# Block-sparse attention and a feed-forward layer on one core: attention in 64x64 quadrants of the TensorE array

## The chip, the cores and the metric

One core of a Trainium2 chip. The time is the device time of one execution in microseconds (us), and a kernel's time is the median of its runs. TensorE is called PE, its weight loads PEld, VectorE DVE, ScalarE ACT, GpSimd POOL and SyncE SP. PEclk is the clock that the throttle granted to PE: 1.0 is full speed, 0.5 half.

## The reference, cut to what matters

```python
# q, k, v: 4 batches x 8 heads x 768 positions x 64, float32
scores_l = q @ k.T / 8                      # kept where |i - j| < 16
scores_s = q @ k_sum.T / 8 + log(32)        # k_sum: maximum over blocks of 32 keys
a = softmax(concat([scores_l masked, scores_s]))
attn = a @ concat([v, v_sum])               # v_sum: mean over blocks of 32 keys
x = attn, heads side by side                # 3072 x 512
h = x @ w_in                                # 512 -> 2048
out = (h * clip(h + 3, 0, 6) / 6) @ w_out   # 2048 -> 512
```

## The kernel before

The feed-forward layer (`hp`, `op`) is the bulk of PE's work: 912 products with full 128x128 weights. Attention is laid between its steps by a hand-made plan of slots. A head is 64 wide, half of PE's rows, so the kernel puts two heads (a pair `p`) on the 128 rows and keeps them apart with block-diagonal operands, half of them zeros: `kbd`, `vbd`, `obd`.

```python
def Sl(b, p, lo, hi):                       # local scores of one pair
    sp = ps_s.tile([128, 512], F32, tag="s", name="sl")
    for i in range(hi - lo):
        t = lo + i
        nc.tensor.matmul(sp[:, i*WIN:(i+1)*WIN], kbd[p][:, t], qT[p][:, ...], start=True, stop=True)
    nc.scalar.activation(a, sp[...], AF.Exp, scale=scl)
    nc.vector.tensor_tensor(a, a, mask, op=ALU.mult)
# [...] Ss: scores with the block summaries, `ss`; exponentials `asum`
def AV(b, p, half):                         # x of one pair, half of the sequence
    nc.tensor.matmul(num[:], vst[p], asm[:], start=True, stop=False)       # block sums of v
    for i, (t, lo, hi, off) in enumerate(bl):                              # 7 key blocks
        nc.tensor.matmul(num[:, lo:hi], vbd[p][:, t], a[:, t, off:off+hi-lo], ...)
    nc.tensor.matmul(den[:], osum[p % 2], asm[:], start=True, stop=False)
    # [...] three products of a with the block-diagonal ones obd, into den
    nc.scalar.activation(lg[:], den[:], AF.Ln)
    nc.scalar.activation(lg[:], lg[:], AF.Exp, scale=-1.0)
    nc.vector.tensor_tensor(xt[s][:, p], num[:], lg[:], op=ALU.mult)
```

The start is written out by hand. `K` and `Tq` transpose k and q of a pair on PE, `busy` are warm-up products on zeros, and `vsum0` makes the block sums of v for the first batch on PE, from float32 (`vps`). The sums need only v, so they sit where q and k of the next pair are still on their way:

```python
K(0, 0)
busy(busy_n, 4)
Tq(0, 0, 0)
vsum0(0)                      # 12 float32 products, 24 instructions in the trace
vcast(0)
K(0, 1)
S_first(0)
vsum0(1, 0, NK // 2)
Tq(0, 1, 0)
vsum0(1, NK // 2, NK)
# [...] pairs 2 and 3 in the same way, then AV(0, 0..3, 0)
```

For later batches DVE makes the sums from v's rows, which come in one transfer for four heads: 4 x 24 blocks on 96 partitions.

```python
def load_vrows(b, g):
    vr_t[b, g] = ld.tile([RS, PCS, w + 8], F32, tag="vr", name="vr", bufs=2)       # RS = 96
    nc.gpsimd.dma_start(out=vr_t[b, g][:, :, 0:w],
                        in_=v[b, 4*g:4*g + 4].rearrange("h (n c t) d -> (h n) c (t d)", c=PCS, n=NB))
```

The softmax here doesn't subtract the row's maximum and nothing guards it: scores larger than these inputs give would overflow.

## Time and profile before

| | before |
|---|---|
| median of 4 runs | 250.66 us (250.37 to 250.72) |
| span of the profiled run | 248.7 us |
| first dense product (`hp`) starts | 25.48 us |
| from there to the last matmul (244.63) | 219.2 us |
| granted clock | 1.0 from 6.9 us to the end of the work |
| busy: PE, DVE, ACT | 236.2, 151.4, 162.2 us |

The table is to be read in two pieces. Up to 25.48 us the core loads, transposes and makes the first x; nothing dense can run before that, so a microsecond lost there is a microsecond of the whole. After it PE is the bound, and attention's instructions count only by the PE time that they take between dense products, and by the waits that they bring. The prediction below shows the lines for both. One more line, of the DMA part of the page (target and source, queue, kind, number, KB each, median us to landing):

```profile
vr<-in_v_dram POOLq DMA_DIRECT2D x6, 768.0 KB, 9.0
```

### The profile page before, as it was taken

To read this page: it belongs to the slowest core of one execution; us is meant where nothing else is said; L and a number is where in the kernel's file an instruction comes from. 1 tells how busy PE (TensorE), PEld (TensorE's weight loads), DVE (VectorE), ACT (ScalarE), POOL (GpSimd) and SP (SyncE) were. 2 spreads that over 40 slices of the span, in tenths; PEclk is the share of its full clock that TensorE was granted. 3 is DMA by queue.
4 is the path that set the end of the run, shared out by engine and by line. 5 is a ranking of instruction groups with operands and counts; after the bars stand their busy time and mean duration, and the time that the engine had idled before them with its cause. 6 is when DMAs were issued, how large, how long until landed. Compare 5 with 4: busy or idle time off the path is not lost.

```text
span 248.7 us, 5021 instructions
## 1 busy us (share of the span) xinstructions
PE 236.2 (95%) x1927; PEld 139.5 (56%) x1950; DVE 151.4 (61%) x354; ACT 162.2 (65%) x316; POOL 67.4 (27%) x101
## 2 busy tenths in 40 slices
PE   7999999999999999769999999999999999999993
PEld 2897566445555656445655555566565555555553
DVE  5598576325579749999863977766444544444300
ACT  8587798427968879865866565777765555555411
POOL 8655005626950216596341200000000000000000
PEclk9999999999999999999999999999999999999999
DMA  6999998999999699999999912110110111111012
GB/s 120 203 173 205 206 193 132 205 248 157 223 155 162 190 213 102 133 128 224 139 180 138 104 33 76 42 45 3 43 42 3 42 42 45 42 42 41 19 71 84
DMA packets 75448, 28.90 MB, mean 116 GB/s; under 512 B 63904, under 2 KB 71328, under 8 KB 75424
## 3 DMA queue, kind: packets, MB, share of 16 engines
q0 software_dynamic: 52752, 17.57, 62.0%
q1 hardware_dynamic: 22672, 11.01, 19.4%
q8 instruction: 15, 0.25, 0.4%
q14 instruction: 9, 0.07, 0.1%
HBM read 31.98 MB, written 6.29 MB: 154 GB/s over the span
## 4 chain that ended last, share of the span: by engine, by line
PE 69%; DVE 19%; ACT 5%; DMA 3%; issue 2%; ACTq 0%; DVEq 0%; POOLq 0%
PE op L443 27%; PE hp L426 26%; DVE g L430 4%; PE num L395 3%; PE sl L357 2%; PE num L393 2%; DVE red L322 2%; DMA kb<-in_k_dram 2%; DVE red L301 2%; ACT r L429 2%; DVE x L413 2%; PE ss L367 2%; PE den L399 2%; DVE kbd L300 2%; DVE kbd L318 2%
## 5 line engine op out<-in xcount | busy, mean ns | idle before, releaser
L426 PE MATMUL hp<-x,win 128*128 128x384 bf16 x512 | 103.2, 326 | 2.0 <-DVE g L430 1.8
L429 ACT ACTIVATE r<-hp,half_c 128x384 f32<-128x384 f32 x128 | 73.2, 580 | 46.4 <-PE hp L426 43.6
L430 DVE SCALAR_TENSOR_TENSOR g<-r,hp 128x384 bf16<-128x384 f32 x128 | 69.8, 552 | 52.2 <-ACT r L429 51.9
L443 PE MATMUL op<-wout,g 128*128 128x512 bf16 x345 | 93.5, 379 | 1.2 <-issue 0.3
L426 PEld LDWEIGHTS <-win 128*128 128x128 bf16 x512 | 47.7, 97 | 37.7 <-issue 5.4
L443 PEld LDWEIGHTS <-g 128*128 128x128 bf16 x368 | 35.2, 98 | 30.7 <-issue 0.6
L413 DVE TENSOR_TENSOR x<-num,lg 128x384 bf16<-128x384 f32 x32 | 17.8, 556 | 21.4 <-ACT lg L412 19.7
L120 POOL DMA_DIRECT2D vbd<-in_v_dram x24 | 18.1, 762 | 33.7 <-PE num L395 21.2
L411 ACT ACTIVATE lg<-den 128x384 f32<-128x384 f32 x32 | 15.7, 492 | 14.8 <-PE den L409 7.2
L360 ACT ACTIVATE at<-sl 128x376 bf16<-128x376 f32 (+2 forms) x48 | 22.2, 486 | 3.9 <-PE sl L357 3.7
L361 DVE TENSOR_TENSOR at<-at,mask 128x376 bf16<-128x376 bf16 (+2 forms) x48 | 16.2, 349 | 2.6 <-ACT at L360 2.3
L412 ACT ACTIVATE lg<-lg 128x384 f32<-128x384 f32 x32 | 16.8, 525 | 0.8
L447 ACT COPY ot<-op 128x512 f32<-128x512 f32 x23 | 13.2, 586 | 5.9 <-PE op L443 5.7
L357 PE MATMUL sl<-qT,kbd 128*128 128x94 bf16 x192 | 14.6, 206 | 2.0 <-DVE kbd L300 1.2
L357 PEld LDWEIGHTS <-kbd 128*128 128x128 bf16 x192 | 11.7, 98 | 8.3 <-issue 1.9
L395 PEld LDWEIGHTS <-vbd 128*128 128x128 bf16 x224 | 12.9, 98 | 5.3 <-issue 1.6
L113 POOL DMA_DIRECT2D qb<-in_q_dram x16 | 13.5, 868 | 5.3 <-DMA vr<-in_v_dram 4.2
L395 PE MATMUL num<-at,vbd 128*128 128x94 bf16 (+2 forms) x224 | 14.1, 199 | 0.0
L113 POOL DMA_DIRECT2D kb<-in_k_dram x16 | 13.6, 883 | 0.0
L402 PE MATMUL den<-at,obd 128*128 128x384 bf16 x32 | 10.7, 333 | 0.5 <-DVE at L361 0.5
L393 PE MATMUL num<-asum,vst 96*128 96x384 bf16 x32 | 10.5, 327 | 0.5 <-DVE x L413 0.3
L399 PE MATMUL den<-asum,osum 96*128 96x384 bf16 x32 | 10.4, 325 | 0.0
(83 smaller groups left out, 204.7 us busy)
## 6 DMA issues: line engine op xcount, KB each, us to landing
out_dram<-ot SPq DMA_DIRECT2D x23, 256.0 KB, 2.3
vr<-in_v_dram POOLq DMA_DIRECT2D x6, 768.0 KB, 9.0
vbd<-in_v_dram POOLq DMA_DIRECT2D x24, 96.0 KB, 4.9
win<-in_moe_w_in_dram POOLq DMA_DIRECT2D x4, 512.0 KB, 9.2
wout<-in_moe_w_out_dram POOLq DMA_DIRECT2D x4, 512.0 KB, 17.0
vf<-in_v_dram SPq DMA_DIRECT2D x8, 192.0 KB, 7.2
kb<-in_k_dram POOLq DMA_DIRECT2D x16, 96.0 KB, 6.2
qb<-in_q_dram POOLq DMA_DIRECT2D x16, 96.0 KB, 6.2
```

The costliest lines, as they stand in the source:

```text
L113: nc.gpsimd.dma_start(out=t[:, :, j], in_=src[b, 2 * p + j].rearrange("(s p) d -> p s d", p=128))
L120: nc.gpsimd.dma_start(out=vall[rows, p, lo:hi, rows], in_=v[b, 2 * p + j].rearrange("(n k) d -> k n d", k=KB)[:, lo:hi])
L357: nc.tensor.matmul(sp[:, i * WIN:(i + 1) * WIN], kbd[p][:, t], qT[p][:, PAD - HALO + t * KB:PAD - HALO + t * KB + WIN], start=True, stop=True)
L360: nc.scalar.activation(a, sp[:, 0:n * WIN].rearrange("p (n c) -> p n c", c=WIN), AF.Exp, scale=scl)
L361: nc.vector.tensor_tensor(a, a, mask[:].unsqueeze(1).to_broadcast([128, n, WIN]), op=ALU.mult)
L395: nc.tensor.matmul(num[:, lo:hi], vbd[p][:, t], a[:, t, off:off + hi - lo], start=False, stop=(i == len(bl) - 1))
L412: nc.scalar.activation(lg[:], lg[:], AF.Exp, scale=-1.0)
L413: nc.vector.tensor_tensor(xt[s][:, p], num[:], lg[:], op=ALU.mult)
L426: nc.tensor.matmul(hp[:], w_in_sb[:, kt, ft * 128:(ft + 1) * 128], xt[t][:, kt], start=(kt == 0), stop=(kt == NP - 1))
L429: nc.scalar.activation(r[:], hp[:], AF.Relu, bias=half_c[:], scale=1.0 / 6.0)
L430: last_g[0] = nc.vector.scalar_tensor_tensor(gt[t][:, ft], r[:], 1.0, hp[:], op0=ALU.min, op1=ALU.mult)
L443: nc.tensor.matmul(op[:], gt[t][:, ft, ts * 128:(ts + 1) * 128], w_out_sb[:, ft], start=(ft == 0), stop=(ft == NFT - 1))
```

## The change

Intent: use the 128x128 array as four 64x64 quadrants, one head each, so that no product multiplies zeros, and the block-diagonal copies need not be made. Four heads are one group `g`. Each row half of the array writes its own PSUM bank. With that go one instruction for twice the columns on ACT, a rearranged order of the start, and v's rows in 32-row places, because the summaries of a head now sit at multiples of 32 partitions.

```diff
 def Sl(...):
-    sp = ps_s.tile([128, 512], F32, tag="s", name="sl")
+    sp = ps_a.tile([128, 2, 512], F32, tag="a", name="sl")
     for i in range(n):
-        nc.tensor.matmul(sp[:, i*WIN:...], kbd[p][:, t], qT[p][:, ...])
+        for r, c in QUAD:                     # ((0,0), (1,1), (0,1), (1,0))
+            p = 2 * g + (r + c) % 2
+            nc.tensor.matmul(sp[quarter(c), r, i*WIN:...], kT[p][quarter(r), t*KB:...], qT[p][quarter(r), ...])
 # AV becomes AVd (den, Ln, Exp) and AVn (num, x), each for a group; in both
+    for c in range(2):                        # block sums: 64 rows x 128 columns
+        nc.tensor.matmul(num[:, c, 0:HALF], vst[b % 2][g][quarter(c)], asm[quarter(c)], start=True, stop=False)
+    for i, (t, lo, hi, off) in enumerate(bl): # values: quarters
+        for r, c in QUAD:
+            nc.tensor.matmul(num[quarter(r), c, lo:hi], vb[b % 2][quarter(c), 2*g + r, t], a[quarter(c), r, t, ...])
 def load_vrows(b, g):
-    nc.gpsimd.dma_start(out=vr_t[b, g][:, :, 0:w], in_=v[b, 4*g:4*g + 4]...)
+    for i in range(4):
+        nc.gpsimd.dma_start(out=vrow[g][SR*i:SR*i + NB, :, 0:w], in_=v[b, 4*g + i]...)
 # the start
 K(0, 0)
 busy(busy_n, 4)
 Tq(0, 0, 0)
-vsum0(0)
 K(0, 1)
-S_first(0)
-vsum0(1, 0, NK // 2)
 Tq(0, 1, 0)
-vsum0(1, NK // 2, NK)
+S_first(0)
 K(0, 2)
 Tq(0, 2, 0)
+vsum0(0)                                      # 24 float32 products, 48 instructions in the trace, 128 weight columns
 Ss(0, 0, 0, HALF)
 K(0, 3)
 Tq(0, 3, 0)
+AVd(0, 0, 0)
+S_first(1)
+vsum0(1)                                      # 24 more
 # [...] then Ss, AVn(0), AVd(1), AVn(1)
```

Cut: the vb and kT buffers, the transposes in groups, the slots of the plan.

## The prediction

> **What bounds the kernel now.** I read the page's busy shares and chain first, then the groups by shape, then TensorE (PE) in order of time, then busy time by stage.
>
> ```profile
> PE 236.2 (95%) x1927; PEld 139.5 (56%) x1950; DVE 151.4 (61%) x354; ACT 162.2 (65%) x316; POOL 67.4 (27%) x101
> ...
> PE 69%; DVE 19%; ACT 5%; DMA 3%; issue 2%; ACTq 0%; DVEq 0%; POOLq 0%
> ```
>
> PE is 95% busy and 69% of the chain that ended last. DVE's 19% of the chain says that some stages hang on VectorE.
>
> ```profile
> L426 PE MATMUL hp<-x,win 128*128 128x384 bf16 x512 | 103.2, 326 | 2.0 <-DVE g L430 1.8
> L443 PE MATMUL op<-wout,g 128*128 128x512 bf16 x345 | 93.5, 379 | 1.2 <-issue 0.3
> ...
> L357 PE MATMUL sl<-qT,kbd 128*128 128x94 bf16 x192 | 14.6, 206 | 2.0 <-DVE kbd L300 1.2 <-ACT at L360 0.8
> ```
>
> Matmuls overlap, so the busy column double counts: what one costs is the step from its start to the next start. A merged row of n matmuls gives it as (length - one duration)/(n-1).
>
> ```profile
> 34.43 0.37 PE L357 MATMUL sl<-qT,kbd 128*128 128x94 bf16 x5
> 34.64 0.81 PE L426 MATMUL hp<-x,win 128*128 128x384 bf16 x4
> ```
>
> That is (370-206)/4 = 41 ns for 94 columns and (810-326)/3 = 161 ns for 384: 2.4 columns a nanosecond. The dense part is then 512 x 0.162 = 83 us plus 384 x 0.216 = 83 us (368 matmuls of 512 columns and 32 halves; 23 records are missing in the count above), 166 us together, and the change does not touch it. One call of the attention's second product (one head pair, half the sequence) is read from its neighbours' starts:
>
> ```profile
> 24.61 0.33 PE L393 MATMUL num<-asum,vst 96*128 96x384 bf16 x1
> 24.78 0.42 PE L395 MATMUL num<-at,vbd 128*128 128x79 bf16 x7
> 25.06 0.32 PE L399 MATMUL den<-asum,osum 96*128 96x384 bf16 x1
> 25.22 0.34 PE L402 MATMUL den<-at,obd 128*128 128x384 bf16 x1
> ...
> 25.48 3.26 PE L426 MATMUL hp<-x,win 128*128 128x384 bf16 x16
> ```
>
> 25.48 - 24.61 = 0.87 us, 32 times: 27.8 us. Local scores: 192 x 0.0417 = 8.0 us. Summary scores: 32 x 0.162 = 5.2 us. So 41.0 us of PE stream is what the change may shrink. Transposes, the float32 block sums of v and warm-up matmuls make some 17 us more; the rest is waits at both ends and in one stage:
>
> ```profile
> core 0: us, PE busy (x) PEld busy (x) DVE busy (x) ACT busy (x) POOL busy (x), PEclk, DMA share, GB/s
> 6.06:25.50 19.44, 18.94 (x309) 16.33 (x310) 15.50 (x35) 14.75 (x29) 11.16 (x22) 1.00 1.18 194
> ...
> 96.00:112.00 16.00, 12.83 (x114) 7.95 (x113) 15.80 (x41) 12.03 (x27) 13.47 (x18) 1.00 1.68 128
> ```
>
> From 96 to 112 us DVE is busy 15.80 of 16 us and PE is idle for 3.2. In the start, up to the first dense matmul at 25.48, PE is nearly full.
>
> **What the skill says.** (1) "TensorEngine Tiling (Array Packing)", Key Properties: tiles work independently, but changing the tiling mode drains the engine. The trace agrees: the 64-column transposes already are such a mode.
>
> ```profile
> 32.66 0.81 PE L426 MATMUL hp<-x,win 128*128 128x384 bf16 x4
> 33.40 0.43 PE L348 MATMUL tp<-ident,qb 36*64 36x36 bf16 x16
> 33.76 0.82 PE L426 MATMUL hp<-x,win 128*128 128x384 bf16 x4
> ```
>
> The last hp starts at 33.47 - 0.33 = 33.14 and the transposes at 33.40: 0.26 us where 0.162 is usual. They end at 33.83, so the last starts near 33.65, and hp follows at 33.76: 0.11 for 0.016. **A switch costs about 0.095 us each way.** (2) "TensorE: Matmul & The Clock Gate", Part 3: tiles of different rows and columns run concurrently, starts some 4 ns apart. The trace shows it for two column halves: 16 transposes of 96 columns in 0.53 us of 218 ns each are 20.8 ns apart, half of the 41 ns that 96 columns stream. Four at once no row of this kernel shows. (3) Same page, Weight-path perf modes: the fast weight load needs 128 columns and no float32. In the trace, 36- and 60-column transposes with 64-column weights still take about 32 ns a pair, so a weight load of 64 columns has a floor near that, under the 41 ns that it must hide behind. (4) "PSUM", bank collisions: two row tiles may not write one bank and quadrant. The diff gives each row half its bank; I take it as correct.
>
> **The change part by part.**
>
> *Stream.* 192 score matmuls become 384 quarter ones, 224 value ones 448, the ones-products 192, summary scores 80 narrow ones, and the 64 products with block sums each have half the contraction. With four tiles at once, 41.0 us becomes 20.5. Of the 20.5 saved, 2.6 lies in the start (4 of 32 second products 3.5 us, 28 of 192 scores 1.2, 4 of 32 summaries 0.65, half of 5.3), leaving **-17.9 us** later. If weight loads of the two row halves follow each other (4 x 16 = 64 ns a group) the later saving is some 5 us less.
>
> *Switches.* Counting changes of rows-by-columns mode down the two PE instruction orders: before 38 (all about transposes), after 196, since each score piece, each summary and each den and num call sits between dense matmuls, and inside den and num there is one more (64x128, then 64x64). In the start 12 becomes 17, later 26 becomes 179: 153 x 0.095 = **+14.5 us**. This eats most of the stream gain. If the inner change is free, it is 3 us less.
>
> *ACT and DVE.* The diagonal copies go (DVE 22 x 0.40 to 0.96, 12.2 us; ACT some 8 us, against 8 full copies of about 0.8 back), the masked kst products (20 x 0.18 = 3.2 us) go, vst halves (16 x 0.28 to 8). Exp, Ln and Exp take 752 or 768 columns at once; at the 0.88 ns a column that lies between 376 (487 ns) and 470 (562), a merged one saves about 0.16 us, some 50 times. Both run under PE and are worth nothing there, except in the 96 to 112 stage, where DVE bound: about 4 us less DVE per batch there frees nearly all of PE's 3.2 us: **-3 us**. The two double-bank buffers now serve scores, den, num and transposes in turn: a wait of +1 us in all.
>
> *The start.* It is on the path: PE runs in order and nothing dense can begin before the first x. Here the order changes: before, block sums filled the wait for q and k from HBM.
>
> ```profile
> 8.19 2.25 PE L274 MATMUL vps<-vf,ind 128*96 128x64 f32 x24
> 10.37 0.53 PE L309 MATMUL tp<-ident,kb 96*64 96x96 bf16 x16
> ...
> 14.66 0.44 PE L348 MATMUL tp<-ident,qb 60*64 60x60 bf16 x16
> ...
> 27.80 2.00 ACT L429 ACTIVATE r<-hp,half_c 128x384 f32<-128x384 f32 x4 [1.00 <-PE hp L426]
> ```
>
> After, all of them come behind the third pair's q. That load is issued at 5.34 us and the longest q load took 9.2 to land: 14.5. PE is mostly idle from 8 to 14.5 us. From there in order: transposes 0.9, two block sums of 48 records (2250-249)/23 = 87 ns now, 104 by my estimate with 128 weight columns for 96, so 5.0 each (4.2 if not), summaries 0.6, two den 0.9, one num 0.45, scores 0.6, about 14 switches 1.3, a wait of 0.8 on the copies of the fourth pair: 15.5 us, first dense matmul at 30.0 (28.4). Then the group's Ln and Exp of 768 columns (2 x 0.85) and two products for x (2 x 0.556) stand between den and the first whole hp: first r near 32.5, against 27.80. **+4.5 us**, between 3 and 6.
>
> *Sum:* 250.7 + 4.5 - 17.9 + 14.5 - 3 + 1 = 249.8. The change has been fitted slot by slot, which speaks for waits tuned a little better than I can see: **249 us**.
>
> **Rivals.** (a) *Packing wins*: switches hide behind waits that are there anyway, or the change between row-tiled modes is free, and the start is filled by loads landing sooner. For it: 54 of the switches end a 64x64 piece beside possible PSUM waits. Against: the trace's switches came at full price in a busy stream. It gives 241 to 244 us. (b) *Packing fails*: quarters with their own weights don't run four at once, only two, so the streams take as long as before (nothing shows four at once). Then -17.9 shrinks to about -9 and the time is 257 to 259. (c) *The start costs nothing*: if the order found more to do before 14.5 us; that gives 245. Against it: the order has the block sums behind that transpose. (d) *DVE or ACT becomes the bound*: against, both get less work.
>
> **Range and chances.** Four terms of 3 to 6 us uncertainty each, partly independent, make about 6 us of spread: 241 to 257. Faster by over 2% means under 245.7: two of the terms have to fall well, 0.27. Slower means over 255.7, mainly rival (b) or a start of +6 with full switches: 0.17. Within 2%: 0.56.
>
> **What would show it.** Right: score quarters start in fours some 42 to 50 ns apart from group to group; each hp-to-quarter and quarter-to-hp step is 0.09 to 0.1 us over the stream; attention's PE stream is about 21 us; first r at 31 to 34 us; DVE busy drops by some 15 us; PE idle in the third-tile stage disappears. Wrong: groups 64 to 80 ns apart (weight loads or two at a time), switch gaps near zero, or the first r at 28 us or before.

## The result, and the profile after

| | before | after |
|---|---|---|
| median (4 runs each) | 250.66 us (250.37 to 250.72) | 266.91 us (265.92 to 267.70) |
| span of the profiled run | 248.7 | 266.0 |
| first dense product | 25.48 | 42.96 |
| first `r` | 27.80 | 47.51 |
| last matmul | 244.63 | 261.99 |
| first dense product to last matmul | 219.2 | 219.0 |
| mean granted clock | 1.0 | 0.921 |
| busy: DVE, ACT | 151.4, 162.2 | 133.2, 147.5 |

The ratio is 1.065 (95% interval 1.061 to 1.069): 6.5% slower. A ratio here is the mean time of one kernel's fast runs over that of the other's of the same rounds, so it is not quite the ratio of the medians quoted. Executions over 1.5% slower than the fastest of the same kernel are left out of the means. All four runs after are with a clock of 0.921 to 0.928: the lower clock belongs to the kernel, not to a state of the chip.

The table already says where the time is: the start became 17.5 us longer, and what follows took as long as before. From the page of the changed kernel (busy by engine; the clock in 40 slices of 6.65 us; the chain that ended last; the issues of v's rows):

```profile
PE 247.7 (93%) x2482; PEld 136.7 (51%) x2510; DVE 133.2 (50%) x301; ACT 147.5 (55%) x242; POOL 78.0 (29%) x114
...
PEclk9655555999999999988999999999999999999999
...
PE 78%; DMA 10%; DVE 4%; ACT 3%; issue 2%; POOL 1%; ACTq 0%; POOLq 0%
...
vr<-in_v_dram POOLq DMA_DIRECT2D x24, 192.0 KB, 10.2
```

PE is *busier* than before (247.7 for 236.2 us) although it has less to stream. Slices 2 to 7 of the clock row give the reason: half speed. Busy time by stage of the changed kernel (columns: stretch and its length, PE, PEld, DVE, ACT, POOL busy with counts, PEclk, DMA share, GB/s):

```profile
8.00:16.00 8.00, 4.36 (x95) 3.70 (x96) 3.38 (x8) 4.25 (x8) 4.33 (x5) 0.56 1.17 212
16.00:24.00 8.00, 8.00 (x40) 8.00 (x39) 0.23 (x1) 0.77 (x2) 5.70 (x8) 0.50 1.11 173
...
32.00:40.00 8.00, 8.00 (x39) 8.00 (x39) 0.68 (x2) 0.38 (x1) 0.00 (x0) 0.50 1.13 186
40.00:48.00 8.00, 8.00 (x113) 3.82 (x112) 2.34 (x5) 2.63 (x5) 0.00 (x0) 0.59 0.02 4
```

And PE in order of time (start, length, engine, line, operation, count, idle before and what ended it):

```profile
9.83 0.85 PE L287 MATMUL tp<-ident,kb 96*64 96x96 bf16 x16 [2.14 <-DMA kb<-in_k_dram]
...
15.37 10.50 PE L262 MATMUL vps<-vf,ind 128*128 128x64 f32 x48
...
30.00 10.50 PE L262 MATMUL vps<-vf,ind 128*128 128x64 f32 x48
...
42.96 0.82 PE L413 MATMUL hp<-x,win 128*128 128x384 bf16 x2
```

PE waits 2.14 us for k of the second pair, and the clock falls to 0.5 at 8.9 us. Then it stays there. The two groups of block sums, started at half clock, take 10.50 us each, with PE busy for 8.00 us of 8. A float32 product is two instructions in the trace, 48 for the 24 products of a group, and they are 213 ns apart. Only when dense products have run from 42.96 on does the clock come back, at 46.5. The kernel before, whose block sums filled those waits, shows the sums 85 ns apart and a clock that never fell.

Later, in the middle of the changed kernel (PE in order of time again):

```profile
96.23 0.82 PE L430 MATMUL op<-wout,g 128*128 128x512 bf16 x3
96.98 0.36 PE L320 MATMUL sl<-qT,kT 64*64 64x94 bf16 x16
97.32 0.34 PE L363 MATMUL den<-asum,osum 64*128 64x384 bf16 x2
97.59 0.45 PE L370 MATMUL den<-at,ones 64*64 64x384 bf16 x12
...
113.66 0.23 PE L320 MATMUL sl<-qT,kT 64*64 64x94 bf16 x2
118.60 0.52 PE L320 MATMUL sl<-qT,kT 64*64 64x94 bf16 x14 [4.70 <-DMA qT<-qb]
```

The upper four lines are the change as intended: 16 quarter products in 0.36 us. Singly, these start at 96.977, .981, .984 and .987, then again in fours at 97.044, 97.087 and 97.129: four at once, and 42 to 43 ns to the next four (67 for the first), as predicted. The switches cost what was predicted too: the last `op` starts at 96.23 + 0.82 - 0.379 = 96.67 and the first quarter 0.31 us later, where 0.216 is the stream, so 0.093; from the two 64x128 products to the quarters it is 0.263 (97.329 to 97.592) where 0.162 is the stream, 0.10. **The inner switch is not free.** The lower two lines are new: a stall of 4.70 us for q's transposes, during which the clock falls again (0.5 from 118.2 to 121.6 us).

Added up over both PE instruction orders after the first dense product, each product being taken to the next start, and at a change of mode its columns at 2.4 a nanosecond: attention's stream went from 36.6 to 20.5 us, and the excess at changes of mode from 3.5 us (26 changes) to 19.8 us (178). So the quadrants saved 16.0 us of stream and paid 16.3 us of switches.

### The profile page after: what moved, and what is told of

The parts are those of the page before. It is cut to its first block, busy times and chain, and to the rows that moved or that the text cites. A ratio compares the mean times of both kernels' runs of the same rounds, so it can differ in the third digit from the quotient of the medians.

```text
span 266.0 us, 6017 instructions
## 1 busy us (share of the span) xinstructions
PE 247.7 (93%) x2482; PEld 136.7 (51%) x2510; DVE 133.2 (50%) x301; ACT 147.5 (55%) x242; POOL 78.0 (29%) x114
## 3 DMA queue, kind: packets, MB, share of 16 engines
q1 hardware_dynamic: 22672, 11.01, 20.5%
## 4 chain that ended last, share of the span: by engine, by line
PE 78%; DMA 10%; DVE 4%; ACT 3%; issue 2%; POOL 1%; ACTq 0%; POOLq 0%
PE hp L413 29%; PE op L430 28%; PE vps L262 8%; DMA vb<-in_v_dram 6%; DMA qb<-in_q_dram 4%; PE tp L287 2%; PE num L397 2%; PE sl L320 2%; PE den L370 2%; PE den L363 2%; PE ss L337 1%; DVE g L417 1%; PE num L393 1%; ACT ot L434 1%; POOL kb L105 1%
## 5 line engine op out<-in xcount | busy, mean ns | idle before, releaser
L138 POOL DMA_DIRECT2D vb<-in_v_dram x24 | 18.1, 756 | 20.8 <-DMA vr<-in_v_dram 12.6
L323 ACT ACTIVATE at<-sl 128x752 bf16<-128x752 f32 (+2 forms) x24 | 19.0, 799 | 8.0 <-PE sl L320 7.7
L400 DVE TENSOR_TENSOR x<-num,lg 128x384 bf16<-128x384 f32 x32 | 16.3, 552 | 10.0 <-PE num L397 6.5
L262 PE MATMUL vps<-vf,ind 128*128 128x64 f32 x96 | 21.0, 422 | 0.0
L262 PEld LDWEIGHTS vps<-vf,ind 128*128 128x128 f32 x96 | 20.6, 332 | 0.2
L326 DVE TENSOR_TENSOR at<-at,mask 128x376 bf16<-128x376 bf16 (+2 forms) x48 | 14.7, 349 | 12.0 <-ACT at L323 11.4
L381 ACT ACTIVATE lg<-den 128x768 f32<-128x768 f32 x16 | 13.0, 811 | 11.8 <-PE den L370 11.6
L152 POOL DMA_DIRECT2D vr<-in_v_dram x24 | 14.2, 596 | 12.9 <-DVE at L326 4.4
L340 ACT ACTIVATE asum<-ss 128x768 bf16<-128x768 f32 (+1 forms) x10 | 6.9, 685 | 19.6 <-PE ss L337 19.6
L320 PE MATMUL sl<-qT,kT 64*64 64x94 bf16 x384 | 10.6, 224 | 5.9 <-DMA qT<-qb 4.7
L382 ACT ACTIVATE lg<-lg 128x768 f32<-128x768 f32 x16 | 13.4, 837 | 0.1
L300 DVE TENSOR_REDUCE kst<-kT 128x24 bf16<-128x768 bf16 x12 | 11.4, 948 | 1.5 <-ACT kT L295 1.2
## 6 DMA issues: line engine op xcount, KB each, us to landing
vr<-in_v_dram POOLq DMA_DIRECT2D x24, 192.0 KB, 10.2
```

Of the source, the lines that this page charges most:

```text
L138: nc.gpsimd.dma_start(out=vb[b % 2][64 * c:64 * c + 64, u], in_=keys_of_v(b, u, c))
L262: nc.tensor.matmul(vps[g][:], ind[:, o:o + 128], vf[2 * g + r][:, n], start=(r == 0 and n == 0), stop=(r == 1 and n == NK - 1))
L320: nc.tensor.matmul(sp[quarter(c), r, i * WIN:(i + 1) * WIN], kT[p][quarter(r), t * KB:(t + 1) * KB], qT[p][quarter(r), PAD - HALO + t * KB ...
L323: nc.scalar.activation(a, sp[:, :, 0:n * WIN], AF.Exp, scale=scl)
L326: nc.vector.tensor_tensor(a, a, mask[:].unsqueeze(1).to_broadcast([128, n, WIN]), op=ALU.mult)
L400: nc.vector.tensor_tensor(xt[s][:, 2 * g + c], num[:, c, 0:HALF], rec[b, g, half][:, c], op=ALU.mult)
```

## The experiments

Two questions. **What made the start so long?** Theory C, the clock: the waits left open by the new order let the clock fall, and float32 sums at half clock don't bring it back. Rivals: O, the order alone (the sums wait for the third pair's q and nothing else fits there), and W, the sums are dear of themselves (float32, 128 weight columns for 96). **What made the stall?** Theory V, v's rows in 24 small transfers make k and q of the next batch come late, by holding up POOL's queue or the transposes issued beside them. Rival K: k's single buffer `kT`.

The expectations of the first four runs use other letters: A is the clock, B says that a long float32 stream lets the clock fall by itself, and C there is W here. Eleven kernels ran.

### e1_warm: keep PE busy in the waits

```diff
 Tq(0, 0, 0)
+fill(8)          # warm-up products on zeros, into an attention buffer
 K(0, 1)
 Tq(0, 1, 0)
+fill(3)
 S_first(0)
+fill(1)
 K(0, 2)
+fill(4)
```

> The changed kernel with 16 more warm-up matmuls put where TensorE waited for loads between 8 and 14.5 us; all else as it was. Theory A (the idle time drops the granted clock, and the float32 sums then run at half speed): clock 1.0 through the start, sums about 107 ns apart for 213, first dense matmul at 29 to 31 us for 42.96, total 252 to 255 us. Theory B (the long float32 stream itself lets the clock fall, whatever came before): the clock is 1.0 when the sums begin and falls inside them, total 258 to 264. Theory C (128 weight columns of float32 cost that much at any clock): sums stay about 213 ns apart with clock 1.0, total 265 to 267.

Correct. 256.31 us (254.88 and 257.74), ratio 1.023 (0.997 to 1.049): some 10 us of the 16 come back. First dense product at 35.04 for 42.96. PE in order of time, and busy time by stage, of this kernel:

```profile
15.18 5.57 PE L262 MATMUL vps<-vf,ind 128*128 128x64 f32 x48
...
23.80 8.77 PE L262 MATMUL vps<-vf,ind 128*128 128x64 f32 x48
```

```profile
15.18:20.75 5.57, 5.57 (x57) 5.50 (x56) 1.02 (x2) 1.29 (x2) 5.57 (x8) 1.00 1.02 151
20.60:25.50 4.90, 4.24 (x99) 3.43 (x99) 1.66 (x4) 4.39 (x8) 1.07 (x2) 1.00 1.24 205
25.50:33.00 7.50, 7.50 (x45) 7.08 (x44) 1.41 (x5) 0.81 (x2) 0.00 (x0) 0.52 1.24 204
```

The same 48 instructions take 5.57 us at clock 1.0 (112 ns apart) and 10.50 at 0.5. So the clock is the larger part of the start: theory C. The second group was not saved: in the stage before it PE is busy 4.24 us of 4.90, in short pieces of quarters, and at 25.7 us, 1.9 us into the second sums, the clock falls once more. 112 ns is 8% over the predicted 104; W is true in size, 112 for 85 ns of the kernel before, but is only 96 x 27 ns = 2.6 us. Start and total are later than expected (29 to 31 us, 252 to 255) because the second group stayed slow. That is the profiled run, 257.74 us at a mean clock of 0.964; the other, 254.88, had 0.992, so there most of this second fall was missing, but it left no profile. That group also fits theory B, a float32 stream that cools the clock by itself; the first, 5.57 us at 1.0, does not, and the clock falls without such a stream too: at 19.4 us in e2, before the second sums begin, and at 21.7 us in e7 below, whose sums are bf16. Whether float32 sums count for less in keeping the clock up was not tested.

### e2_order: the first group's sums back in their old places

```diff
 Tq(0, 0, 0)
+vsum0(0, (0,))
 K(0, 1)
 Tq(0, 1, 0)
+vsum0(0, (1,))
 S_first(0)
 K(0, 2)
 Tq(0, 2, 0)
-vsum0(0)
```

> The changed kernel with the first group's block sums put back where the kernel before had them, half behind the first q transposes and half behind the second; the second group's 48 stay together. Theory A (idle time drops the clock): clock mostly 1.0, first dense matmul at 27 to 30 us, total 250 to 254. Theory B (a float32 stream lets the clock fall): the clock falls in the second group's sums, if not in the first, and total is 255 to 262. If the order of the start is not what costs: 264 to 267.

Correct. 256.95 us (256.55 and 257.35), ratio 1.025 (1.014 to 1.036). The first group's two halves take 2.89 us each, 111 to 112 ns apart, at clock 1.0; the second group again 10.50 us, since the clock fell at 19.4 us in the broken stage before it. First dense product at 33.21. The total lies in the range for theory B, but not for B's reason, since the clock fell before those sums. Order and warm-ups give nearly the same: what counts most is that PE is kept busy, with whatever work. O keeps a share. In e1 the order is the change's, and of its 9.6 us over the kernel before (35.04 for 25.48) the second sums' half clock is 3.2 (8.77 for 5.57) and the half clock of the work behind them perhaps 1.2; by this estimate some 5 us stay with the order and the dearer sums together, near the 4.5 that the prediction gave to its start.

### e3_bf16: the sums from bf16

```diff
-ind = const.tile([128, ZI + 128], F32, tag="ind", name="ind")
+ind = const.tile([128, ZI + 128], BF16, tag="ind", name="ind")
-    nc.tensor.matmul(vps[g][:], ind[:, o:o + 128], vf[2 * g + r][:, n], ...)
+    nc.tensor.matmul(vps[g][:], ind[:, o:o + 128], vb[0][:, 2 * g + r, n], ...)
 # and the casts to vb ahead of the sums
```

> The changed kernel with the block sums of batch 0 as bf16 matmuls on the already cast v, in the same places. Theories A and B both: 48 sums take 1.7 to 3 us a group for 10.5, first dense matmul at 27 to 29 us, total 248 to 252. If the start is late for its loads and its order and not for the sums: first dense matmul later than 35 us and total over 258.

Correct (the sums in PSUM stay float32; v is rounded). 255.77 us (254.56 and 256.98), ratio 1.021 (0.998 to 1.043). The clock is at 0.5 from 10.4 to 30.8 us, but a bf16 sum is one instruction, 24 for a group, and they are 53 ns apart; the first dense product starts at 28.73, 14.2 us sooner than in the changed kernel and where it was expected (27 to 29). The total was not (248 to 252). The time moved by 11 only, because the stall in the middle is larger here, 8.65 us between two starts. The wait list of this kernel (who waited for what: us in total, times, longest):

```profile
POOL vb L138 <- DMA vr<-in_v_dram: 17.3, 10, 3.9
...
PE sl L320 <- DMA qT<-qb: 8.4, 1, 8.4
```

So a shorter start alone does not mend the change. The stall does not simply grow as the start shrinks: with starts of 35.04 (e1) and 33.21 (e2) the longest one was 3.49 and 2.28 us.

### e4_before_late: the kernel before, with its sums late

The position alone, without a single quadrant: in the kernel before, the block sums of pairs 0 and 1 go behind the third pair's q.

```diff
 Tq(0, 0, 0)
-vsum0(0)
 vcast(0)
 K(0, 1)
 S_first(0)
-vsum0(1, 0, NK // 2)
 Tq(0, 1, 0)
-vsum0(1, NK // 2, NK)
 # [...]
 Tq(0, 2, 0)
+vsum0(0)
+vsum0(1)
 # pairs 2 and 3 likewise in one piece
```

> The kernel before with one part of the change alone: the block sums moved behind the third pair's q transposes, both pairs of a group together; its attention stays in block-diagonal form and its sums keep 96 weight columns. Theories A and B: the clock falls to 0.5 there too, sums go from 85 to about 160 ns apart and the total rises by 8 to 15 us. If the 128-column weights or the quarters are needed for the loss: under 4 us more.

Correct. Two runs, 262.01 and 266.60, which is slow, so there is no ratio; the fast one is 11.2 us over the 250.85 us median of the fast runs of the kernel before. PE in order of time:

```profile
10.31 0.85 PE L309 MATMUL tp<-ident,kb 96*64 96x96 bf16 x16 [2.11 <-DMA kb<-in_k_dram]
...
15.91 7.94 PE L274 MATMUL vps<-vf,ind 128*96 128x64 f32 x48
...
28.36 5.07 PE L274 MATMUL vps<-vf,ind 128*96 128x64 f32 x48
```

The same wait, the same fall of the clock (9.6 us), the sums at 160 to 165 ns for 85. After the full-array attention from 25.1 us on the clock comes back, at 30.1 us, 1.7 us into the second group, which ends at 85 ns. First dense product at 37.06 for 25.48, which is 11.6 us, and from there to the last matmul 219.19 for 219.16. **The order of the start alone costs the kernel before 11 us**, with no quadrant in it. Of these, 4.1 us are the moved work itself, the first group's 48 instructions of 85 ns, which had run inside the waits before 14.66 us (rival O); the other 7.5, by this estimate, come with the half clock. So theory C is shown as the larger cause, and O as a smaller one.

### f1_kt2, f2_novr, f3_vr96: the stall, by three cuts

All three start from e3, whose stall is the largest.

```diff
 # f1: k's transposes in two sets of buffers, by parity of the batch
+kT2 = [[const.tile([128, S], BF16, ...) for p in range(NP)] for i in range(2)]
-    X(kT[p][:], kb_t[b, p][0])
+    X(kT2[b % 2][p][:], kb_t[b, p][0])
 # f2: v's rows of batches 2 and 3 not loaded (wrong on purpose)
-    at_slot(rows, lambda g=g: load_vrows(b + 1, g))
 # f3: v's rows in one transfer per group on 96 partitions, not in 32-row places (wrong on purpose)
-    for i in range(4):
-        nc.gpsimd.dma_start(out=vrow[g][SR*i:SR*i + NB, :, 0:w], in_=v[b, 4*g + i]...)
+    nc.gpsimd.dma_start(out=vrow[g][0:4*NB, :, 0:w], in_=v[b, 4*g:4*g + 4]...)
```

> The changed kernel with bf16 block sums (as e3_bf16) and the transposed k in two buffers by turns, which the kernel before had and the change took away with its copies. Theory K (the transposes of batch 2 start late because the single buffer of k is still being read): the stall of 8.4 us before the first scores of batch 2 goes or falls under 2 us, total 246 to 249. Theory V (the transposes are issued in time and land late, behind the loads of v's rows in pieces of 24 partitions): stall stays 5 to 9 us, total 253 to 257.

> As e3_bf16, but v's rows for batches 2 and 3 are not loaded again (wrong result on purpose: the block sums of batch 1 stand in). Theory V: the transposes then land in about 5 us, the stall before the first scores of batch 2 falls under 2 us, total 243 to 248. Theory K: the stall stays, total 252 to 256.

> As e3_bf16, but each group's rows of v come in one transfer onto 96 partitions, the kernel before's shape, in place of four onto 24 each (wrong result on purpose, the sums then add the wrong rows; bytes, readers and arithmetic are the same). Theory V in its form of pieces (it is the number of transfers, 24 for 6, that blocks the queue and delays the loads of k and q and their transposes): stall under 2 us, total 243 to 248. If it is the bytes of these rows: stall and total as in e3_bf16, 253 to 257.

| | time, us | ratio | stall in the middle (start to start) | clock 0.5 after the start |
|---|---|---|---|---|
| f1_kt2, correct | 253.72 (253.43 to 255.02) | 1.013 (1.010 to 1.017) | 5.67 | 100.7 to 107.5 |
| f2_novr, relative error 4.66 | 247.74 (247.64 to 247.97) | 0.989 (0.986 to 0.991) | none over 1.3 | none |
| f3_vr96, relative error 0.70 | 248.83 (248.06 to 250.13) | 0.993 (0.989 to 0.997) | none over 1.94 | none |

f3 moves as many bytes of v as the change does, in a quarter of the transfers; its page says

```profile
vr<-in_v_dram POOLq DMA_DIRECT2D x6, 768.0 KB, 12.4
```

and the stall is gone, with the half clock after it. A transfer of 192 KB on 24 partitions takes a median of 10.2 us to land, one of 768 KB on 96 takes 9.0 before and 12.4 here: four times as many transfers are four times as many landings. That is theory V: it is the rows in small transfers that make the stall.

By which of its two ways, f2 tells. The queue is held up in the changed kernel: POOL waits eight times, 12.6 us in all, for a landing of v's rows before it may issue the next v block, and the first k of batch 2 is issued at 81.6 us, 38.6 after the first dense product, where the kernel before issues it 33.4 after. But in f2 it is issued nearly as late, 37.4 after (e3: 38.0), and there is no stall; and in f3, without a stall too, POOL waits longer for v's rows (10.2 us before v blocks, 6.0 before q loads). What f2 lacks is the next round of row transfers, which the changed kernel issues beside the transposes of q (POOL and SP in order of time):

```profile
99.01 4.72 POOL L152 DMA_DIRECT2D vr<-in_v_dram  x8 [3.59 <-DVE at L326]
101.31 1.23 SPq L270 DMA_TRANSPOSE qT<-qb  x1
```

This transpose landed 17.2 us after its issue, at 118.5 us, and PE went on at 118.60. The same one landed after 20.4 us in e3 and after 7.7 in f2; in f3 it is issued ahead of the rows and lands after 6.6. So the stall is a late landing, and not the late issue of k. K is not shown: f1's second buffer did not move the transposes (the one that PE waits for is issued 58.4 us after the first dense product, in e3 58.3), and its 3.0 us less stall are a landing after 17.0 us for 20.4, in one profile each. By the ranges f1 and f2 fell where V had them (253 to 257, 243 to 248), and f3 0.8 us above its 248. Why a quarter of the bytes takes as long to land (fewer partitions at a time, or the queue) was not told apart.

f3 also shows what the quadrants are worth when the rest is out of the way: from its first dense product to the last matmul it takes 214.9 us for 219.2, 4.3 us less, with a stream of 20.0 us and an excess at 174 switches of 18.3.

### e7_all: the start and the switches together

e3, e1's warm-ups, f1's buffers, and the products with block sums in quarters too, so that the inner switch falls away:

```diff
-    for c in range(2):
-        nc.tensor.matmul(num[:, c, 0:HALF], vst[b % 2][g][quarter(c)]..., asm[quarter(c)], ...)
+    for r, c in QUAD:
+        nc.tensor.matmul(num[quarter(r), c, 0:HALF], vst[b % 2][g][quarter(c), r], asm[quarter(c)], ...)
```

> The changed kernel with bf16 block sums, warm-up matmuls in the waits of the start, k in two buffers, and the products with block sums in four quarters each (32 tiling switches fewer, worth 3 us if each costs 0.095). All repairs right: first dense matmul at 25 to 27 us, no stall, total 238 to 243 us. Theory V alone right about the stall: 246 to 251. Switches hidden behind other waits: 3 us more than that.

Correct. 251.12 us (250.68 to 252.33), ratio 1.003 (0.999 to 1.007), as fast as before and no more, just above the 246 to 251 that were expected if only the stall stayed. It still has v's rows in 24 transfers, and a stall of 6.77 us at 97.1 us with half clock from 100.3 to 107.1.

### g0_place, g1_place_q, g2_pairs: a correct kernel without the small transfers

g0 keeps f3's single transfer and brings the 24 sums of each head to their 32-row places with one small product:

```diff
+    nc.gpsimd.dma_start(out=vrow[b, g][:, :, 0:w], in_=v[b, 4*g:4*g + 4]...)   # 96 partitions, two buffers
 def vsum(b, g):
     # [...] DVE adds as before, the last into bf16 `o`
+    nc.tensor.matmul(sp[:, 0, 0:D], spread[:], o[:], start=True, stop=True)      # 96 x 128 selection
-    to_vst(b, g, r[:, 0, 0:D])
+    to_vst(b, g, sp[:, 0, 0:D])
```

with bf16 sums (the second group behind the second `den`), e1's warm-ups and f1's buffers. g1 is g0 with e7's quarters for the block sums. g2 is g1 with `AVn` directly behind `AVd`, which saves the two switches between them.

> A correct repair: the changed kernel with bf16 block sums in batch 0 (the second group's now behind the second den), warm-up matmuls in the waits, k in two buffers, and v's rows of later batches in one transfer of 96 partitions into double-buffered tiles, their sums spread to the 32-row places by one small matmul. If the start and the pieces were all that was wrong: first dense matmul at 25 to 27 us, no stall over 2 us, rest 215 us as in f3_vr96, total 243 to 247. If the stall comes back by another transfer: 248 to 252.

> As g0_place, with one thing more: each product with block sums in four quarters in place of two 64x128 halves, so that 32 calls have no tiling switch inside. Stream time is the same by the trace (halves and quarters of 384 columns both start together). Switches cost 0.1 us each on the path: 2.5 to 3.5 us less than g0_place. Switches hidden behind other waits: under 1 us less.

> As g1_place_q, with each num call put right behind its den call instead of two dense steps later, which takes away up to two switches for each of the 14 pairs. Switches on the path: 2 to 3 us less than g1_place_q. If holding both double banks at once makes the scores wait: the same or up to 3 us more.

| all correct | time, us | ratio | switches after the first dense product, excess | first dense product to last matmul |
|---|---|---|---|---|
| g0_place | 249.50 (248.85 to 249.58) | 0.996 (0.995 to 0.998) | 162, 17.3 us | 217.6 |
| g1_place_q | 246.76 (244.90 to 247.64) | 0.985 (0.980 to 0.991) | 129, 13.4 us | 215.3 |
| g2_pairs | 248.77 (246.13 to 249.60) | 0.992 (0.986 to 0.998) | 107, 11.1 us | 216.8 |

g0 missed the 243 to 247 us that were hoped for: its first dense product is at 26.19, as expected, but the stretch is 217.6 for 215. g1 is faster than both kernels: 1.5% under the kernel before, with an interval that leaves open whether it reaches 2%. From g0 to g1 33 switches fewer take 3.9 us off the excess, 2.3 off the stretch and 2.7 off the time, inside the 2.5 to 3.5 expected if a switch is paid in full. From g1 to g2 another 2.3 us of excess goes, and the stretch grows by 1.5: `den` and `num` back to back need both PSUM buffers at once, and waits (gaps over 0.9 us or so between starts) rise from 4.6 to 6.4 us. g2 is a miss of the expectation that each switch taken away is worth its price. What is left in g1 is a wait of another kind (PE in order of time):

```profile
107.86 0.32 PE L420 MATMUL hp<-x,win 128*128 128x384 bf16 x1 [2.68 <-DVE g L424]
```

DVE is held by the sums of v's rows and the masks in this stage and gives `g` late; the clock falls for 3.4 us after it (108.2 to 111.6).

## Why the prediction was wrong

The predicted time was 249 us (241 to 257), the measured one 266.9. By its steps:

| step | predicted | measured |
|---|---|---|
| start, to the first dense product | 30.0 (first `r` 32.5) | 42.96 (47.51) |
| stream after the start | -17.9 | -16.0 |
| switches after the start | +14.5 | +16.3 |
| DVE-bound stage, and waits on the shared buffers | -3 and +1 | with the stall, about -0.5 together |
| after the start, in all | -5.4 | -0.2 |

**The step that failed is "The start".** It foresaw the order, and even the moment: "PE is mostly idle from 8 to 14.5 us", transposes of 0.9, so sums from 15.4 on; they began at 15.37. Then it charged the sums at "104 by my estimate with 128 weight columns for 96, so 5.0 each", a full-clock number. They took 10.43 and 10.42 us to the next start, which is 10.9 us over the estimate. The remaining work up to the first dense product, 5.5 us by the prediction with the transposes, took 2.1 more than it should, also at half clock. 10.9 + 2.1 is the whole of 42.96 - 30.0. From the first dense product to the first `r` it was 4.55 for 2.5, with 3.5 of the 4.55 us at half clock.

What it lacked was one inference. Its own table of stages quotes a clock of 1.00, and it used that as a constant of the chip, while it wrote in the same paragraph that PE would stand idle. For idle time of that length the Trainium skill has a warning: "TensorE: Matmul & The Clock Gate", in the section "Why this matters for your kernels", asks for "No PE-idle gaps >~3µs between matmul bursts". The longest wait came to 2.14 us only, and the clock fell some 1.2 us into it. PE was then busy 4.36 us of 8, and the clock stayed at 0.5. e1 and e4 show it from both sides: the same order with filled waits has the first sums at full speed, and the kernel before with open waits loses 11 us, some 7 of them by the clock.

**The stream** was right: four at once, 42 to 43 ns from group to group, stream 20.5 us after the start where the prediction implied 17.9. The 1.9 us missing from the gain are perhaps small gaps in the quarters, such as the 67 ns after the first four; they were not added up. **The switches** were right in price, 0.093 to 0.10 us, inner ones included; 178 were counted for 179, and with the waits at them they cost 1.8 us more.

**DVE and ACT** fell by 18.2 and 14.7 us; some 15 had been said of DVE. (The 0.88 ns a column of the prediction's ACT part should be 0.80 by its own figures, (562 - 487)/94; nothing hangs on it.) The DVE-bound stage did not go: in f3, where no stall covers it, DVE is busy 15.83 us of 16 from 96 to 112 us, and PE 14.00, for 15.80 and 12.83 before, so that of the 3 us promised some 1.2 came. And the +1 us "wait in all" missed the transfers, the second step that failed. The diff shows `for i in range(4)` around the loads of v's rows; the prediction did not price it, since no transfer was on the path before. It became a stall of 4.7 us and a cold clock behind it, and took back what the rest had won. f3 puts that number right: without the stall the stretch is 4.3 us shorter, near the predicted 5.4.

**The rivals.** (b), quarters that don't run four at once, came nearest in size (257 to 259), for a reason that is shown false. (c), a start that costs nothing, was the wrong way round. None of the four had the clock in it. The range took the four terms as errors of a few us each about a working at full clock; a change of regime was not among them.

**What stays open**: whether k's single buffer has any part in the stall; and why the float32 sums at half clock do not raise it (below).

## What to carry to other kernels

Before an order is changed, look at what the old one did for the clock: work that seems movable may be what keeps PE busy while the loads land, and a wait there cost twice, once itself and once through everything that runs at half clock until dense products come back. Splitting the array pays only for as long as PE stays in the mode: here 16 us of stream were bought for 16 us of switches, and the profit came from putting neighbouring products into the same mode (33 switches fewer, 1.1% of the time). And count the transfers that a new layout needs: the same bytes in four times as many issues delayed the transposes issued beside them, which had not been on the path.

## What the Trainium skill lacked or had wrong

- "TensorE: Matmul & The Clock Gate", Part 1: the table there has the clock come back after some 3.4 us of sustained busy time. Here 10.5 us of float32 products, PE busy 8.00 us of 8, stayed at 0.5 from beginning to end, twice in the changed kernel and once in e2; the same stream begun at 1.0 kept 1.0 for 5.57 us in e1's first group, and lost it 1.9 us into the second. The clock rose 1.0 to 3.5 us after the first dense bf16 products (42.96 to 46.5; 35.04 to 36.0; 33.21 to 36.5). Why is open.
- The same page, "Why this matters for your kernels": gaps of about 3 us are named as the limit. That row alone would not have warned of these runs: in the changed kernel the clock fell some 1.2 us into a wait of 2.14, and in e2 at 19.4 us, where no gap since 15 us had passed 0.9 us but PE was busy for 2.44 us of 4.40.
- "TensorEngine Tiling (Array Packing)", Key Properties: a change of mode drains the engine, without a figure. The runs show 0.093 to 0.10 us for each change, from 128x128 to 64x64 (0.31 for 0.216) and from 64x128 to 64x64 (0.263 for 0.162).
- No page that I found says that a float32 product is two instructions in the trace, or how they are spaced at half clock: 160 to 165 ns with 96 weight columns and 213 with 128 (85 and 112 at full clock), for 64 columns that stream. The same sums from bf16 are one instruction each, 53 ns apart at half clock.
- "DMA: Bandwidth & Descriptors", Bandwidth: its rule speaks of the size of a transfer. The runs add that transfers of 192 KB on 24 partitions took as long to land (10.2 us) as those of 768 KB on 96 (9.0 and 12.4), and that a transpose issued among eight of them landed after 17.2 us, and after 7.7 us where they were left out (f2).
